# A decode layer on one core: half of the V loads move to a second DMA queue, and a selector matmul goes from the tail

## The chip, the cores and the metric

The kernel runs on one core of a Trainium2 chip. The core has a matrix engine (TensorE, PE in the profile), three engines for element-wise work (VectorE or DVE, ScalarE or ACT, GpSimd or POOL), a sync engine that here only issues transfers (SyncE, SP), and 16 DMA engines that move data between the device memory and the core's own memory. The metric is the device time of one execution in microseconds. Three runs of the kernel before gave 203.14, 202.99 and 204.5; the median is 203.14.

## The reference, cut to what matters

One token goes through one transformer layer: an attention block with a cache of 4096 positions in 32 heads, and a gated feed-forward block, each with a layer norm ahead and a residual sum behind.

```python
x = A_x                                              # [1, 1, 640]
# A: q = ln(x) @ wq -> 32 heads of 128; k_cache, v_cache: [1, 32, 4096, 128]
s = einsum("bhqd,bhkd->bhqk", q, k) * 128 ** -0.5
o = einsum("bhqk,bhkd->bhqd", softmax(s), v)
h = x + o.reshape(1, 1, 4096) @ wo                   # wo: [4096, 640]
# B: w_gate, w_up: [640, 1728], w_down: [1728, 640]
g, u = ln(h) @ w_gate, ln(h) @ w_up
out = h + (gelu(g) * u) @ w_down                     # gelu in its tanh form
```

Everything is bfloat16. The K and V caches are 32 MB each, the weights some 16 MB together, and each byte is used once.

## The kernel before, in words

**Groups and slots.** The 32 heads are taken in eight groups of four, so K of a group (K0 to K7) and V of a group (V0 to V7) are 4 MB each, laid out as 128 partitions of 32 KB. They go through three buffers of the core's memory, `slot0` to `slot2`. The list `order` (lines 170 to 173) is K0, V0, K1, then K(G+1), V(G) for G from 1 to 6, and V7; the n-th entry uses slot n % 3. `consumed[n]` is the event at which entry n has been read to its end: for K the last of four multiplies of VectorE (line 273), for V the last matmul of `pv_group` (line 310). A load of entry n waits for `consumed[n - 3]`. So V2, for example, goes into K2's slot, and K4 into V1's.

**Issue.** `issue` (line 183) writes the loads into SyncE's instruction list, in the order of `order`. Each engine works its list off in order, and a transfer that waits for a slot holds back what stands behind it in the same list. All loads of K, V and the weights are issued by SyncE, on its one DMA queue; ScalarE issues only x, at the start, on its own.

**Attention.** For each K group, `scores` makes four units of 32 positions per partition. VectorE multiplies K by q (line 273), TensorE folds the products with an identity (line 281), VectorE sums the rest (line 288), and ScalarE takes the exponentials in four parts (line 292). VectorE's list has the reduction of a unit behind the multiply of the next one. For each V group, `pv_group` multiplies the exponentials with V on TensorE (line 310), and ScalarE copies the result out (line 314). V of a group comes one K group later in the order than its own K, so TensorE takes V(G) behind the folds of K(G+1).

**Tail.** Behind V7, SyncE's list has w_o in three parts (from the arena that held w_q), then w_down's last rows, w_gate, w_up in two parts, and the rest of w_down in four. `proj_part`, the second layer norm, `glu` and the GELU follow each part. The 1728 rows of w_down make 13 and a half blocks of 128. The last half block, rows 1664 to 1727, is loaded as halves of rows on 128 partitions; the 64 GLU values that belong to it stand on partitions 0 to 63 of column 13, and a matmul with the selector `sel2` (line 451) with a multiply by `par` (line 453) spreads them into `hm2`. The last block of `down` reports one event for each of four output pieces of 160 columns (line 459), which VectorE and ScalarE copy to `out_row`.

Of the kernel before, what the change touches and what calls it, by code (L numbers as in the profile page):

```python
# [5 lines left out]
FP32 = mybir.dt.float32  # L6
BF16 = mybir.dt.bfloat16
ALU = mybir.AluOpType
ACTF = mybir.ActivationFunctionType
AX = mybir.AxisListType  # L10
# [10 lines left out]
NG = 8  # L21
NSLOT = 3
# [79 lines left out]
def bass_sequential_preLN__gqa_block_cached__glu_gated_geglu__decode_kernel(nc, A_x, A_k_cache, A_v_cache, A_wq, A_wo, B_x, B_w_gate, B_w_up, B_w_down, out):  # L102
    sb = lambda name, shape, dt: nc.alloc_sbuf_tensor(name, shape, dt)
# [10 lines left out]
    out_row = sb("out_row", [1, D], BF16)  # L114
# [5 lines left out]
    hlnT = sb("hlnT", [128, 5], BF16)  # L120
# [10 lines left out]
    e_t = sb("e_t", [128, 14], FP32)  # L131
    gu = sb("gu", [128, 14], FP32)
    hm = sb("hm", [128, 14], BF16)
    hm2 = sb("hm2", [128, 2], BF16)
    sel2 = sb("sel2", [64, 64, 2], BF16)
    par_t = sb("par_t", [128, 2, 64], BF16)
    par = sb("par", [128, 2], FP32)
    one_bf = sb("one_bf", [1, 1], BF16)
    ones_f = sb("ones_f", [128, 128], FP32)
    mean_f = sb("mean_f", [128, 128], FP32)  # L140
    ones_b = sb("ones_b", [128, 1024], BF16)
# [6 lines left out]
    ps_g, ps_u = bank[0], bank[1]  # L148
    ps_q = [bank[3], bank[7]]
    ps_a = bank[3]  # L150
    ps_d = bank[3][:, 256:416]
    ps_o = [bank[2], bank[4]]
    ps_s = bank[5]
    ps_z = bank[6]
# [5 lines left out]
    P = Prog(nc)  # L160
    V = lambda fn, *d: P.op("vector", fn, *d)
    A = lambda fn, *d: P.op("scalar", fn, *d)
    T = lambda fn, *d: P.op("tensor", fn, *d)
    GP = lambda fn, *d: P.op("gpsimd", fn, *d)
# [9 lines left out]
    pos = {t: n for n, t in enumerate(order)}  # L174
    landed, consumed = {}, {}
# [3 lines left out]
    def wo_load(name, t, lo, hi):  # L179
        d_wo[name] = P.dma("sync", wo_sb[:, t, lo:hi, :],  # L180
                           A_wo[2048 * t:2048 * t + 2048, :].rearrange("(p i) n -> p i n", i=16)[:, lo:hi, :], qd)

    def issue(upto):
        while state["next"] < min(upto, len(order)):
            n = state["next"]
            kind, g = order[n]
            src = A_k_cache if kind == "K" else A_v_cache
            src = src[0, 4 * g:4 * g + 4, :, :].rearrange("h (p r) d -> (h p) (r d)", p=32)
            dst = slots[n % NSLOT][:, 0:128 * DH]
            parts = 2 if n == len(order) - 1 else 1  # L190
            w = 128 * DH // parts
            landed[n] = [P.dma("sync", dst[:, i * w:(i + 1) * w], src[:, i * w:(i + 1) * w], consumed[n - NSLOT] if n >= NSLOT else None)
                         for i in range(parts)]
            state["next"] = n + 1

    issue(NSLOT)


# [5 lines left out]
    c_onesb = GP(lambda e: e.memset(ones_b[:, :], 1.0))  # L204
    c_idb = GP(lambda e: e.affine_select(id_b[:, :], ones_b[:, 0:128], pattern=[[1, 128]], compare_op=ALU.is_equal,
                                         fill=0.0, base=0, channel_multiplier=-1), c_onesb)
    c_idf = GP(lambda e: e.affine_select(id_f[:, :], ones_f[:, :], pattern=[[1, 128]], compare_op=ALU.is_equal,
                                         fill=0.0, base=0, channel_multiplier=-1), c_ones)
    c_sel = GP(lambda e: e.affine_select(sel[:, :, :], ones_b[0:16, :].rearrange("p (a b) -> p a b", a=8),
                                         pattern=[[-1, 8], [1, 128]], compare_op=ALU.is_equal,  # L210
                                         fill=0.0, base=0, channel_multiplier=-8), c_onesb)
    GP(lambda e: e.memset(hs[:, :, :], 0.0))
    c_hs = GP(lambda e: e.affine_select(hs_t[:, :, :], ones_f[:, 0:64].rearrange("p (a b) -> p a b", a=4),
                                        pattern=[[-32, 4], [-1, 16]], compare_op=ALU.is_equal,
                                        fill=0.0, base=0, channel_multiplier=1), c_ones)
    c_sel2 = GP(lambda e: e.affine_select(sel2[:, :, :], ones_b[0:64, 0:128].rearrange("p (a b) -> p a b", a=64),
                                          pattern=[[1, 64], [0, 2]], compare_op=ALU.is_equal,
                                          fill=0.0, base=0, channel_multiplier=-1), c_onesb)
    c_par = GP(lambda e: e.affine_select(par_t[:, :, :], ones_b[:, 0:128].rearrange("p (a b) -> p a b", a=2),
                                         pattern=[[-1, 2], [-2, 64]], compare_op=ALU.is_equal,  # L220
                                         fill=0.0, base=0, channel_multiplier=1), c_onesb)
    c_pbd = GP(lambda e: e.memset(p_bd[:, :, :, :], 0.0))
    c_rs = GP(lambda e: e.memset(RS[:, :, :], 0.0))

    c_po = [V(lambda e, b=b: e.memset(bank[b][:, :], 0.0)) for b in (2, 4)]
    c_hs = V(lambda e: e.reduce_sum(hs[:, :, 12:16], hs_t[:, :, :].rearrange("p t (g j) -> p g j t", g=4), axis=AX.X), c_hs)

    V(lambda e: e.reduce_sum(par[:, :], par_t[:, :, :], axis=AX.X), c_par)


    def x_cols(e):
# [35 lines left out]
    folds, reds, exps, pvs, evs, hds = {}, {}, {}, {}, {}, {}  # L267

    def score_mult(s):
        G, n = s // 4, pos[("K", s // 4)]  # L270
        kt = view(n)
        u = s % 4
        m = V(lambda e: e.tensor_tensor(  # L273
            out=prod[:, s % 4, :, :], in0=kt[:, 32 * u:32 * u + 32, :],
            in1=qb[:, G, :].unsqueeze(1).to_broadcast([128, 32, DH]), op=ALU.mult),
            landed[n][0], qa, qc, folds.get(s - 4))
        consumed[n] = m

        def fold(e):
            for b in range(8):  # L280
                i = e.matmul(ps_f[s % 2][:, :], id_b[:, :], prod[:, s % 4, :, 16 * b:16 * b + 16],  # L281
                             start=(b == 0), stop=(b == 7))
            return i
        folds[s] = T(fold, m, c_idb, reds.get(s - 2))
# [59 lines left out]
    def proj_part(t, lo, hi, *ws):  # L344
        def fn(e):
            for c in range(5):
                for i in range(lo, hi):
                    r = e.matmul(ps_p[:, c:c + 1], wo_sb[:, t, i, c::5], aP[:, t, i:i + 1],  # L348
                                 start=(t == 0 and c == 0 and i == 0), stop=(t == 1 and i == 15),
                                 skip_group_check=True)  # L350
            return r
        return T(fn, *ws)

    def scores(G):
        for i in range(4):
            score_mult(4 * G + i)
            if i >= 1:
                score_exp(4 * G + i - 1)
        score_exp(4 * G + 3)
        issue(pos[("K", G)] + 1 + NSLOT)  # L360

    heads = None
    for kind, G in order:
# [7 lines left out]
        if G == 4:  # L371
# [4 lines left out]
    a1 = finish_half(1)  # L376

    wo_load("0", 0, 0, 16)  # L380
    wo_load("1a", 1, 0, 12)
    wo_load("1b", 1, 12, 16)
# [4 lines left out]
    wd_sb = sl[1][:, 0:14 * D].rearrange("p (m n) -> p m n", m=14)  # L387
# [1 line left out]
    wd_v = B_w_down[0:1536, :].rearrange("(a p r) n -> p a r n", a=3, r=4)  # L389
    wd_d = wd_sb[:, 0:12, :].rearrange("p (a r) n -> p a r n", a=3)  # L390
    d_wd = [P.dma("sync", wd_sb[:, 12, :], B_w_down[1536:1664, :], free[1]),
            P.dma("sync", wd_sb[:, 13, 0:320], B_w_down[1664:1728, :].rearrange("f (s n) -> (f s) n", s=2))]
    d_wg = P.dma("sync", wg_sb, B_w_gate[:, :].rearrange("(p c) n -> p c n", c=5), free[0])
    d_wu = [P.dma("sync", wu_sb[:, 0:3, :], wu_v[:, 0:3, :]),
            P.dma("sync", wu_sb[:, 3:5, :], wu_v[:, 3:5, :])]
    d_wd += [P.dma("sync", wd_d[:, a, lo:hi, :], wd_v[:, a, lo:hi, :])
             for a, lo, hi in ((0, 0, 4), (1, 0, 4), (2, 0, 3), (2, 3, 4))]

    V(lambda e: e.memset(ps_g[64:128, 13:14], 0.0), reds[31])
    V(lambda e: e.memset(ps_u[64:128, 13:14], 0.0), reds[31])  # L400
    proj_part(0, 0, 16, a0, d_wo["0"])
    proj_part(1, 0, 12, a1, d_wo["1a"])
    pr = proj_part(1, 12, 16, d_wo["1b"])
    h = V(lambda e: e.tensor_add(hT[:, 0:5], xx[:, 0:5], ps_p[:, 0:5]), pr)  # L404
# [6 lines left out]
    def glu(ps, w, cs):  # L411
        def fn(e):
            for c in cs:
                for m in range(14):
                    ws = w[:, c, 512 * (m // 4) + m % 4:512 * (m // 4) + 512:4] if m < 12 else \
                        w[:, c, 128 * m:min(128 * m + 128, DF)]
                    i = e.matmul(ps[0:128 if m < 13 else 64, m:m + 1], ws, hlnT[:, c:c + 1],  # L417
                                 start=(c == 0 and m == 0), stop=(c == 4), skip_group_check=True)
            return i
        return fn  # L420
# [18 lines left out]
    g6 = V(lambda e: e.tensor_mul(gu[:, :], g_t[:, :], t1[:, :]), g8)  # L439
    g9 = V(lambda e: e.tensor_mul(hm[:, :], gu[:, :], ps_u[:, 0:14]), g6, up)  # L440

    def down(ms, qs=range(4)):
        def fn(e):
            for m in ms:
                for q in qs:
                    h, n = (hm[:, m:m + 1], 160 * q) if m < 13 else (hm2[:, q // 2:q // 2 + 1], 160 * (q % 2))
                    i = e.matmul(ps_d[32 * q:32 * q + 1, 0:160], h, wd_sb[:, m, n:n + 160],  # L447
                                 start=False, stop=(m == 11))
            return i
        return fn  # L450
    hp = T(lambda e: e.matmul(ps_z[:, 0:1], sel2[:, :, :].rearrange("p a b -> p (a b)"), hm[0:64, 13:14],
                              start=True, stop=True), g9, c_sel2)
    h2 = V(lambda e: e.tensor_mul(hm2[:, :], par[:, :], ps_z[:, 0:1].to_broadcast([128, 2])), hp)
    T(down([12]), d_wd[0])
    T(down(range(4)), d_wd[2])
    T(down([13]), h2, d_wd[1])
    T(down(range(4, 8)), d_wd[3])
    T(down(range(8, 11)), d_wd[4])
    dn = {q: T(down([11], [q]), d_wd[5]) for q in (0, 2, 1, 3)}
    os = [V(lambda e, q=q: e.tensor_copy(out_row[0:1, 160 * q:160 * q + 160], ps_d[32 * q:32 * q + 1, 0:160]), dn[q])  # L460
          for q in range(2)]
    os += [A(lambda e, q=q: e.copy(out_row[0:1, 160 * q:160 * q + 160], ps_d[32 * q:32 * q + 1, 0:160]), dn[q])
           for q in range(2, 4)]
    d_out = P.dma("sync", out[0, :, :], out_row[:, :], *os)
    P.op("sync", None, d_out)
# [30 lines left out]
```

## Time and profile before

| What | us |
|---|---|
| time of the profiled execution | 203.14 |
| its span, from the first to the last instruction | 201.9 |
| TensorE busy | 120.4 (60%) |
| VectorE busy | 101.2 (50%) |
| ScalarE busy | 61.1 (30%) |
| GpSimd busy | 5.0 (2%) |
| SyncE's DMA queue, share of the 16 engines' span | 97.8% |
| read from device memory | 84.23 MB, 417 GB/s over the span |

Times in the profile count from the first instruction of the span. The row named DMA gives the mean busy share of the 16 DMA engines in 40 equal slices of some 5 us, in tenths. In the timeline, the first number of a row is its start, the second its length; SPq and ACTq are the transfers that SyncE and ScalarE issue, and the length of such a row is the time that issuing took, not the transfer's. A bracket at the end tells how long the engine sat idle ahead of the row and what released it. In the chain, a DMA row's length runs from its issue to its landing. In the rows of transfers by tile, the last number is the median time from issue to landing.

### The profile page before, as it was taken

To read this page: it belongs to the slowest core of one execution; us is meant where nothing else is said; L and a number is where in the kernel's file an instruction comes from. 1 tells how busy PE (TensorE), PEld (TensorE's weight loads), DVE (VectorE), ACT (ScalarE), POOL (GpSimd) and SP (SyncE) were. 2 spreads that over 40 slices of the span, in tenths; PEclk is the share of its full clock that TensorE was granted. 3 is DMA by queue.
4 is the path that set the end of the run, shared out by engine and by line. 5 is a ranking of instruction groups with operands and counts; after the bars stand their busy time and mean duration, and the time that the engine had idled before them with its cause. 6 is when DMAs were issued, how large, how long until landed. Compare 5 with 4: busy or idle time off the path is not lost.

```text
span 201.9 us, 2505 instructions
## 1 busy us (share of the span) xinstructions
PE 120.4 (60%) x1010; PEld 58.8 (29%) x1010; DVE 101.2 (50%) x106; ACT 61.1 (30%) x273; POOL 5.0 (2%) x14
## 2 busy tenths in 40 slices
PE   0107058537937668690968197727844887467395
PEld 0103023112312233150324032312331344267383
DVE  3201088517979847924791578277708760100221
ACT  2101004620563550670156125603640363100101
POOL 7200000000000000000000000000000000000000
PEclk9999657995799996997599859988995799955555
DMA  9999999999999999999999999999999999999992
GB/s 357 414 404 467 428 415 416 422 448 458 430 415 422 415 445 448 435 424 416 422 435 441 438 435 424 416 428 441 448 419 435 399 425 437 419 408 435 412 409 113
DMA packets 4335, 84.39 MB, mean 418 GB/s; under 512 B 482, under 2 KB 868, under 8 KB 1508
## 3 DMA queue, kind: packets, MB, share of 16 engines
q1 hardware_dynamic: 4322, 84.23, 97.8%
q8 instruction: 8, 0.13, 0.3%
q14 instruction: 3, 0.02, 0.0%
q10 hardware_dynamic: 2, 0.00, 0.0%
HBM read 84.23 MB, written 0.00 MB: 417 GB/s over the span
## 4 chain that ended last, share of the span: by engine, by line
DMA 64%; PE 16%; DVE 14%; issue 3%; SPq 2%
DMA slot<-in_A_k_cache_dram 42%; DVE prod L273 12%; DMA slot<-in_B_w_down_dram 11%; DMA slot<-in_A_v_cache_dram 11%; PE bank L281 11%; PE bank L310 3%; SPq L51 2%; DVE sc L288 2%; PE bank L319 1%; PE bank L447 0%; DVE out_row L460 0%; PE bank L330 0%; DVE RT L329 0%
## 5 line engine op out<-in xcount | busy, mean ns | idle before, releaser
L281 PE MATMUL bank<-prod,id_b 128*128 128x512 bf16 x256 | 75.4, 454 | 50.8 <-DVE prod L273 50.8
L273 DVE TENSOR_TENSOR prod<-slot,qb 128x4096 bf16<-128x4096 bf16 x32 | 72.4, 2285 | 31.1 <-DMA slot<-in_A_k_cache_dram 31.1
L292 ACT ACTIVATE p_bd<-sc,zero_t 32x32 bf16<-32x32 f32 x128 | 46.4, 362 | 86.3 <-DVE sc L288 85.1
L281 PEld LDWEIGHTS bank<-prod,id_b 128*128 128x128 bf16 x256 | 26.9, 113 | 99.4 <-DVE prod L273 63.1
L288 DVE TENSOR_REDUCE sc<-bank 128x32 f32<-128x512 f32 x32 | 22.0, 688 | 21.4 <-PE bank L281 21.4
L292 ACT ACTIVATION_READ_ACCUMULATOR p_bd<-sc,zero_t 32x1 f32 x128 | 23.5, 184 | 0.0
L310 PE MATMUL bank<-slot,p_bd 128*16 128x512 bf16 x256 | 17.3, 379 | 3.1 <-ACT p_bd L292 2.5
L310 PEld LDWEIGHTS bank<-slot,p_bd 128*16 128x16 bf16 x256 | 9.4, 89 | 7.3 <-ACT p_bd L292 3.0
L319 PE MATMUL bank<-po_sb,hs 128*16 128x128 f32 x64 | 8.4, 274 | 1.1 <-ACT po_sb L314 1.1
L348 PE MATMUL bank<-aP,arena 128*128 128x1 bf16 x160 | 6.7, 178 | 3.8 <-DMA arena<-in_A_wo_dram 3.8
L417 PE MATMUL bank<-hlnT,slot 128*128 128x1 bf16 (+1 forms) x140 | 6.7, 176 | 3.2 <-DMA slot<-in_B_w_gate_dram 3.2
L259 PE MATMUL bank<-arena,xlnB 128*32 128x512 bf16 x40 | 3.9, 565 | 7.2 <-DMA arena<-in_A_wq_dram 7.2
L348 PEld LDWEIGHTS bank<-aP,arena 128*128 128x128 bf16 x160 | 6.6, 131 | 3.9 <-DMA arena<-in_A_wo_dram 2.5
L314 ACT COPY po_sb<-bank 128x512 f32<-128x512 f32 x8 | 4.7, 585 | 9.6 <-PE bank L310 9.6
L417 PEld LDWEIGHTS bank<-hlnT,slot 128*128 128x128 bf16 (+1 forms) x140 | 6.3, 118 | 4.1 <-DVE hX L407 3.3
L319 PEld LDWEIGHTS bank<-po_sb,hs 128*16 128x16 f32 x64 | 5.5, 96 | 4.5 <-issue 2.1
L244 ACT ACTIVATE ln<-ln,eps_t 128x1 f32<-128x1 f32 x2 | 0.6, 294 | 20.3 <-DVE ln L242 20.3
L263 DVE CAST qb<-bank 128x512 bf16<-128x512 f32 x1 | 0.7, 692 | 9.6 <-PE bank L259 9.6
L404 DVE TENSOR_TENSOR hT<-xx,bank 128x5 f32<-128x5 f32 x1 | 0.2, 163 | 10.2 <-PE bank L348 10.2
L233 PE MATMUL bank<-one_bf,x_row 1*128 1x1 bf16 x5 | 0.4, 177 | 6.9 <-DMA x_row<-in_A_x_dram 6.9
L259 PEld LDWEIGHTS bank<-arena,xlnB 128*32 128x32 bf16 x40 | 1.6, 136 | 9.1 <-issue 9.0
L334 DVE TENSOR_SCALAR aT<-bank,rz 16x128 bf16<-16x128 f32 x2 | 0.7, 339 | 6.0 <-PE bank L319 6.0
(65 smaller groups left out, 26.3 us busy)
## 6 DMA issues: line engine op xcount, KB each, us to landing
slot<-in_A_k_cache_dram SPq DMA_DIRECT2D x8, 4096.0 KB, 21.4
slot<-in_A_v_cache_dram SPq DMA_DIRECT2D x7, 4096.0 KB, 17.5
arena<-in_A_wq_dram SPq DMA_DIRECT2D x1, 5120.0 KB, 15.4
slot<-in_A_v_cache_dram SPq DMA_DIRECT2D x2, 2048.0 KB, 20.0
arena<-in_A_wo_dram SPq DMA_DIRECT2D x1, 2560.0 KB, 27.3
slot<-in_B_w_gate_dram SPq DMA_DIRECT2D x1, 2160.0 KB, 16.3
arena<-in_A_wo_dram SPq DMA_DIRECT2D x1, 1920.0 KB, 31.5
slot<-in_B_w_up_dram SPq DMA_DIRECT2D x1, 1296.0 KB, 18.4
```

The lines of the kernel that those rows point to most:

```text
L51: ev = self.op(eng, lambda e: e.dma_start(out, in_), *deps, dma=True)
L259: i = e.matmul(ps_q[hf][32 * j:32 * j + 32, :], xlnB[:, c, :], wq_j[:, c, j, 4 * hf:4 * hf + 4, :], start=(c == 0), stop=(c == 4))
L263: qa = V(lambda e: e.tensor_copy(qb[:, 0:4, :].rearrange("p g d -> p (g d)"), ps_q[0][:, :]), qd)
L273: m = V(lambda e: e.tensor_tensor(out=prod[:, s % 4, :, :], in0=kt[:, 32 * u:32 * u + 32, :], in1=qb[:, G, :].unsqueeze(1).to_broadcast([1 ...
L281: i = e.matmul(ps_f[s % 2][:, :], id_b[:, :], prod[:, s % 4, :, 16 * b:16 * b + 16], start=(b == 0), stop=(b == 7))
L288: reds[s] = V(lambda e: e.reduce_sum(sc[:, s % 4, :], ps_f[s % 2][:, :].rearrange("p (g d) -> p g d", d=16), axis=AX.X), folds[s], exps.ge ...
L292: x = A(lambda e, j=j: e.activation(p_bd[32 * j:32 * j + 32, G % 2, 32 * (s % 4):32 * (s % 4) + 32, j], sc[32 * j:32 * j + 32, s % 4, :], ...
L310: i = e.matmul(po[a:a + 16, :], p_bd[:, G % 2, 4 * b:4 * b + 4, :].rearrange("p g j -> p (g j)"), vt[:, 4 * b:4 * b + 4, :], start=(b < 4) ...
L314: evs[G] = A(lambda e: e.copy(po_sb[:, G % 2, :], po[:, :]), pvs[G], hds.get(G - 2))
L319: i = e.matmul(ps_a[0:16, 128 * (G // 4):128 * (G // 4) + 128], hs[:, r, 12 - 4 * g:28 - 4 * g], po_sb[:, G % 2, 128 * r:128 * r + 128], s ...
L348: r = e.matmul(ps_p[:, c:c + 1], wo_sb[:, t, i, c::5], aP[:, t, i:i + 1], start=(t == 0 and c == 0 and i == 0), stop=(t == 1 and i == 15), ...
L417: i = e.matmul(ps[0:128 if m < 13 else 64, m:m + 1], ws, hlnT[:, c:c + 1], start=(c == 0 and m == 0), stop=(c == 4), skip_group_check=True)
```

## The change

V1 to V6 are loaded through ScalarE's queue; K, V0, V7 and all weights stay on SyncE's. The load is written into ScalarE's list at the place where `issue` is called. In `scores`, that call moves from the end to a place behind the fourth multiply, ahead of the exponentials of the third and the fourth unit. The slots and what a load waits for are the same.

The last half block of w_down is loaded as the last 128 rows, 1600 to 1727, of which partitions 64 to 127 are used. `glu` writes its column 13 to these partitions, so the selector, `par`, `hm2` and their instructions are gone, two on GpSimd and one on VectorE at the start among them. Block 13 goes directly behind block 12, and the last block reports one event for all four output pieces.

```diff
@@ issue
-            landed[n] = [P.dma("sync", dst[:, i * w:(i + 1) * w], src[:, i * w:(i + 1) * w], consumed[n - NSLOT] if n >= NSLOT else None)
+            queue = "scalar" if kind == "V" and 0 < g < NG - 1 else "sync"
+            landed[n] = [P.dma(queue, dst[:, i * w:(i + 1) * w], src[:, i * w:(i + 1) * w], consumed[n - NSLOT] if n >= NSLOT else None)
@@ constants
-    c_sel2 = GP(lambda e: e.affine_select(sel2[:, :, :], ones_b[0:64, 0:128].rearrange("p (a b) -> p a b", a=64),
...
-    c_par = GP(lambda e: e.affine_select(par_t[:, :, :], ones_b[:, 0:128].rearrange("p (a b) -> p a b", a=2),
...
-    V(lambda e: e.reduce_sum(par[:, :], par_t[:, :, :], axis=AX.X), c_par)
@@ scores
             score_mult(4 * G + i)
+            if i == 3:
+                issue(pos[("K", G)] + 1 + NSLOT)
             if i >= 1:
                 score_exp(4 * G + i - 1)
         score_exp(4 * G + 3)
-        issue(pos[("K", G)] + 1 + NSLOT)
@@ tail
-            P.dma("sync", wd_sb[:, 13, 0:320], B_w_down[1664:1728, :].rearrange("f (s n) -> (f s) n", s=2))]
+            P.dma("sync", wd_sb[:, 13, :], B_w_down[1600:1728, :])]
...
-    V(lambda e: e.memset(ps_g[64:128, 13:14], 0.0), reds[31])
-    V(lambda e: e.memset(ps_u[64:128, 13:14], 0.0), reds[31])
+    V(lambda e: e.memset(ps_g[0:64, 13:14], 0.0), reds[31])
+    V(lambda e: e.memset(ps_u[0:64, 13:14], 0.0), reds[31])
...
-                    i = e.matmul(ps[0:128 if m < 13 else 64, m:m + 1], ws, hlnT[:, c:c + 1],
+                    i = e.matmul(ps[0 if m < 13 else 64:128, m:m + 1], ws, hlnT[:, c:c + 1],
...
-    hp = T(lambda e: e.matmul(ps_z[:, 0:1], sel2[:, :, :].rearrange("p a b -> p (a b)"), hm[0:64, 13:14],
-                              start=True, stop=True), g9, c_sel2)
-    h2 = V(lambda e: e.tensor_mul(hm2[:, :], par[:, :], ps_z[:, 0:1].to_broadcast([128, 2])), hp)
-    T(down([12]), d_wd[0])
-    T(down(range(4)), d_wd[2])
-    T(down([13]), h2, d_wd[1])
-    T(down(range(4, 8)), d_wd[3])
-    T(down(range(8, 11)), d_wd[4])
-    dn = {q: T(down([11], [q]), d_wd[5]) for q in (0, 2, 1, 3)}
+    T(down([12, 13], False), g9, d_wd[0], d_wd[1])
+    T(down(range(4), False), d_wd[2])
+    T(down(range(4, 8), False), d_wd[3])
+    T(down(range(8, 11), False), d_wd[4])
+    dn = T(down([11], True), d_wd[5])
```

More of the change, by code (lines that the diff above doesn't have):

```diff
@@ L133, in bass_sequential_preLN__gqa_block_cached__glu_gated_geglu__decode_kernel @@
     hm = sb("hm", [128, 14], BF16)
[L134 to L137, printed above, removed]
     one_bf = sb("one_bf", [1, 1], BF16)
@@ L215, in bass_sequential_preLN__gqa_block_cached__glu_gated_geglu__decode_kernel @@
                                         fill=0.0, base=0, channel_multiplier=1), c_ones)
-    c_sel2 = GP(lambda e: e.affine_select(sel2[:, :, :], ones_b[0:64, 0:128].rearrange("p (a b) -> p a b", a=64),
-                                          pattern=[[1, 64], [0, 2]], compare_op=ALU.is_equal,
-                                          fill=0.0, base=0, channel_multiplier=-1), c_onesb)
-    c_par = GP(lambda e: e.affine_select(par_t[:, :, :], ones_b[:, 0:128].rearrange("p (a b) -> p a b", a=2),
-                                         pattern=[[-1, 2], [-2, 64]], compare_op=ALU.is_equal,
-                                         fill=0.0, base=0, channel_multiplier=1), c_onesb)
     c_pbd = GP(lambda e: e.memset(p_bd[:, :, :, :], 0.0))
@@ L440, in bass_sequential_preLN__gqa_block_cached__glu_gated_geglu__decode_kernel, with down @@
     g9 = V(lambda e: e.tensor_mul(hm[:, :], gu[:, :], ps_u[:, 0:14]), g6, up)
-    def down(ms, qs=range(4)):
+    def down(ms, last):
         def fn(e):
             for m in ms:
[L445 to L448, printed above, removed]
-            return i
-        return fn
-    hp = T(lambda e: e.matmul(ps_z[:, 0:1], sel2[:, :, :].rearrange("p a b -> p (a b)"), hm[0:64, 13:14],
-                              start=True, stop=True), g9, c_sel2)
-    h2 = V(lambda e: e.tensor_mul(hm2[:, :], par[:, :], ps_z[:, 0:1].to_broadcast([128, 2])), hp)
-    T(down([12]), d_wd[0])
-    T(down(range(4)), d_wd[2])
-    T(down([13]), h2, d_wd[1])
-    T(down(range(4, 8)), d_wd[3])
-    T(down(range(8, 11)), d_wd[4])
-    dn = {q: T(down([11], [q]), d_wd[5]) for q in (0, 2, 1, 3)}
-    os = [V(lambda e, q=q: e.tensor_copy(out_row[0:1, 160 * q:160 * q + 160], ps_d[32 * q:32 * q + 1, 0:160]), dn[q])
+                k = slice(0 if m < 13 else 64, 128)
+                for q in range(4):
+                    i = e.matmul(ps_d[32 * q:32 * q + 1, 0:160], hm[k, m:m + 1], wd_sb[k, m, 160 * q:160 * q + 160],
+                                 start=False, stop=(last and m == ms[-1]))
+            return i
+        return fn
+    T(down([12, 13], False), g9, d_wd[0], d_wd[1])
[3 more added lines that the diff above has]
+    dn = T(down([11], True), d_wd[5])
+    os = [V(lambda e, q=q: e.tensor_copy(out_row[0:1, 160 * q:160 * q + 160], ps_d[32 * q:32 * q + 1, 0:160]), dn)
           for q in range(2)]
-    os += [A(lambda e, q=q: e.copy(out_row[0:1, 160 * q:160 * q + 160], ps_d[32 * q:32 * q + 1, 0:160]), dn[q])
+    os += [A(lambda e, q=q: e.copy(out_row[0:1, 160 * q:160 * q + 160], ps_d[32 * q:32 * q + 1, 0:160]), dn)
            for q in range(2, 4)]
```

## The prediction

> **What bounds the kernel now.** I read the page's DMA rows first, then the chain that ended last, then the SyncE rows of the timeline. The page:
>
> ```profile
> span 201.9 us, 2505 instructions
> ...
> DMA  9999999999999999999999999999999999999992
> ...
> q1 hardware_dynamic: 4322, 84.23, 97.8%
> ...
> q10 hardware_dynamic: 2, 0.00, 0.0%
> ```
>
> One queue (q1, SyncE's) keeps the 16 DMA engines busy from the first slice to the last but one; ScalarE's queue (q10) carries two packets. No compute engine exceeds 60%. So the kernel ends when its last byte lands, and a change can cost time in three ways only: more bytes, a pause in the stream, or a longer tail behind the last byte. The chain in order of time gives the pace:
>
> ```profile
> 1.65 42.91 DMA slot<-in_A_k_cache_dram
> ...
> 73.81 19.85 DMA slot<-in_A_k_cache_dram
> ...
> 111.10 21.41 DMA slot<-in_A_k_cache_dram
> ...
> 149.22 22.22 DMA slot<-in_A_v_cache_dram
> ...
> 176.80 22.42 DMA slot<-in_B_w_down_dram
> ```
>
> K of group 1 lands at 44.56 (1.65 + 42.91), K of 4 at 93.66, K of 6 at 132.51. Four 4 MB loads lie between the last two (V3, K5, V4, K6), so one takes 38.85 / 4 = 9.71 us; five lie between 44.56 and 93.66 (K2, V1, K3, V2, K4), 9.82 each. Transfers run one behind another without a pause, although SyncE issues each only when a slot comes free:
>
> ```profile
> 43.22 0.33 SPq L51 DMA_DIRECT2D slot<-in_A_v_cache_dram  x1
> 56.43 0.33 SPq L51 DMA_DIRECT2D slot<-in_A_k_cache_dram  x1
> 69.12 0.33 SPq L51 DMA_DIRECT2D slot<-in_A_v_cache_dram  x1
> 73.81 0.33 SPq L51 DMA_DIRECT2D slot<-in_A_k_cache_dram  x1
> ```
>
> ```profile
> 74.25 4.49 DVE L273 TENSOR_TENSOR prod<-slot,qb 128x4096 bf16<-128x4096 bf16 x2 [2.47 <-DMA slot<-in_A_k_cache_dram]
> ```
>
> The first four rows are the issues of V1, K3, V2 and K4; the fifth, VectorE's, is the start on K3 when it lands, at 74.25. V2's issue at 69.12 comes 5.1 us before the stream would run dry at 74.25: that is the cover which the change has to keep. Three more prices follow. K3 is read to its end at 85.82, the issue of V3, 11.6 after it landed (K4 likewise: 93.66 to 105.38, 11.7). V1's slot comes free 73.81 - 69.12 = 4.7 after K2's. And K2, which found VectorE busy with K1, was done 69.12 - 56.43 = 12.7 after it.
>
> **The change, part by part.** *V1 to V6 on ScalarE's queue.* Nothing is added to the bytes here; what changes is the order. In before, V1 is served behind K2, because both are in one queue. After, V1 is issued by ScalarE behind V0's eviction, 43.22 + 0.58, before K1 lands, so K2 and V1 are due at the same moment on two queues. How do the engines serve two queues? The one pair in this trace is x on q10 beside w_q on q1:
>
> ```profile
> 1.29 0.50 ACTq L51 DMA_DIRECT2D x_row<-in_A_x_dram  x1
> ```
>
> ```profile
> L233 PE MATMUL bank<-one_bf,x_row 1*128 1x1 bf16 x5 | 0.4, 177 | 6.9 <-DMA x_row<-in_A_x_dram 6.9
> ...
> arena<-in_A_wq_dram SPq DMA_DIRECT2D x1, 5120.0 KB, 15.4
> ```
>
> x is issued at 1.29, behind w_q (issued at 0.00), and is used at 6.93, while w_q lands at 15.4: the second queue is let in within a transfer of the first. The trace's packet records are finer still: x's data packet runs at 5.00, its 4-byte completion packet at 6.57, and between them fits one w_q packet of 1.51 us. That is taking turns, packet by packet. A V load has as many packets per engine as a K load, of equal size, so I take half of the rate for each.
>
> The Trainium skill bears on both sides of this. "DMA: Bandwidth & Descriptors", section "Queues, rings and completion order", says that an engine goes round its queues in turn and leaves one only after a whole packet, typically 9 to 17 descriptors. If a K load's share of one engine were one such packet, K2 would still land before V1, and the sum below would be +0.2 us. The row of x, let in long before w_q's end, speaks for the fine grain. The same page's section "Issuing engines are not separate DMA queues" says that all queues interleave on the same engines and that a second issuer saves only issue time; by that nothing is gained here, and the loss that I find is not foreseen.
>
> Now the walk. From 44.56, K2 and V1 share two loads' time, 19.4 us. K2 lands at 44.56 + 19.4 = 64.0 if its last packet comes last, at 62.8 if one packet (9.71 / 8 = 1.2) earlier; before, one load behind K1, it was near 54.5. VectorE has been done with K1 since about 59, so it waits. K3, issued at 56.4 on SyncE's queue, follows as the third load and lands at 74.2, as before: the stream is full until there. K2 is read to its end 11.7 after landing, at 74.5 to 75.7, and only then is V2 issued. K4 needs V1's slot, 4.7 later still. So at 74.2 **both queues are empty** and all three slots hold data being read: the 5.1 us of cover become a shortfall of 0.3 to 1.5 us, plus the restart.
>
> The restart r, from issue to the moment from which the load counts at full rate, was hidden and is now in the open. Below: the output's store, 1.2 KB on an idle queue, issued in 0.31 and then awaited by SyncE for 0.8: 1.1 us. Above: w_q, issued at 0.00, landed at 15.4, of which 5.12 MB at the pace above take 12.1: 3.3 us, program start included. V2 is neither; it is a load as large as w_q, in a program already running. I take 2.2. Pause: 75.1 + 2.2 - 74.2 = **3.1 us**, between 74.5 + 1.1 - 74.2 = 1.4 and 75.7 + 3.3 - 74.2 = 4.8.
>
> Does it come again? V2 runs alone from 77.3, K4 (issued at 79.8) joins 4.7 later, so the queues are now out of step: V2 is done at 92.0, K4 at 101.4, V3 at 111.4, and K5 then has 4.7 left, to 116.1. K4 is read out at 113.1; V4 is in flow at 115.3. The cover is 0.8 us, or -0.3 with the long restart. The same step falls again between K7 and V6, near 154. I take 0 for both and leave 0 to 0.6 for the range.
>
> A pause also lets the DMA engine that lags catch up: the five loads up to 93.66 took 49.10 against 5 x 9.71 = 48.55. That is worth 0 to -0.55; I take -0.2.
>
> *ScalarE's six issues.* 0.33 us each as on SyncE, 0.50 as x took: 2 to 3 us in six places. ScalarE waits there for the fourth multiply of a K group, with the exponentials of the third and fourth unit behind it. Those need a reduction that VectorE runs after that same multiply, so the wait costs nothing; an exponential is used only one group later. 0.
>
> *w_down's tail.* The second load grows from 80 to 160 KB: 0.08 MB at 418 GB/s, +0.2 us on the stream. The selector matmul and `hm2` (two steps of 0.18 and 0.16 us) leave a stretch in which PE is waiting for w_down anyway, from 197.24 to the last landings near 199.6: 0. Still 56 matmuls. The last four report one event in place of four; in before the copies started at 200.01 and 200.04 while PE was done at 199.98, so 0 to +0.1, taken at 0.1. The GpSimd and VectorE work taken from the start (0.70, 0.29 and 0.29 us, over by 5.5) ends before x arrives at 6.93: 0.
>
> Sum: 3.1 - 0.2 + 0.2 + 0.1 = **+3.2 us**. The profiled execution took 203.14 for a span of 201.9, and is itself the median of the three runs. Forecast: 203.1 + 3.2 = 206.3.
>
> **Rivals.**
> 1. *K keeps its place* (ends on the other side: not slower). If SyncE's queue gets more than its half, K2 lands earlier. There is no pause if K2 is read out r before 74.2: it must land by 74.2 - 11.7 - 1.1 = 61.4 with the short restart, by 59.2 with the long one. K2's 9.71 us in 16.8 or 14.6 us: a share of 58% to 66%. From there on the price is 0.2 + 0.1: 203.4. For it: a 5.1 us cover to spare. Against it: x's turn-taking.
> 2. *The pause recurs.* K5 and K7 have 0.8 us of cover or less. If a read-out takes 12.7 in place of 11.7 (as back to back), or the restart is the long one, each costs 0.3 to 1.5, on a first pause of 3 to 4.8: +5 to +6, 208 to 209.
> 3. *Two queues fill gaps.* q1 is busy 97.8%; the missing 2.2% are 4.4 us, of which the last slice (at 113 GB/s, some 3.5 us) is the tail that no queue fills. At most 1 us is left: 202.1 with no pause at all. More than 1% faster would need bytes to move faster than 9.71 us a load, for which nothing in the trace speaks.
>
> **How the numbers follow.** One pause as walked: 0.74. Rival 1: 0.11. Rival 2: 0.11. Rival 3, and anything that makes it faster: 0.04. A change of 1%, 2 us, is about what a measurement of this kernel can tell from none (its own runs spread from 202.99 to 204.5). One pause at its low end (1.4 to 1.8) lies within 1%; that is 0.11 of its 0.74. So faster 0.03, same 0.23, slower 0.74. The range runs from rival 1's 203.4 to the top of rival 2, 209.0.
>
> **What would show it.** In the changed profile: V1 and K2 land within 1.5 us of each other near 63 to 64; VectorE waits some 4 us for K2 where it had K2 at hand before; one slice of the DMA row near 74 to 78 falls well below 9, and the GB/s with it; V2's issue on ScalarE's queue at about 75; from there all lags by some 3 us, to the end; the last landing to the end takes no more than 0.2 longer than now. I am wrong if K2 lands by 61 (rival 1), if the DMA row dips at three places (rival 2), or if 4 MB take other than 9.7 us where both queues run.

## The result, and the profile after

The changed kernel takes 209.28 us (median of 6 runs, 208.87 to 211.11) against 203.14 us before: 6.1 us more, a ratio of 1.0303 with a 95% interval of 1.0255 to 1.0351. The forecast was 206.3 with a range of 203.3 to 209.0: the direction was right, the size half of what came, and the time lies just above the range. Medians here are over all runs of a kernel, while ratios leave out runs that lie more than 1.5% above the kernel's fastest, so the two can differ, by up to 0.9%.

The page of the changed kernel, the rows that were read first of before:

```profile
span 208.1 us, 2498 instructions
...
DMA  9999999999999789999999999999979999999992
GB/s 355 394 455 403 447 447 416 409 476 422 405 453 447 321 302 413 460 430 409 447 453 384 384 414 441 441 416 441 428 280 403 409 409 430 426 413 432 409 410 101
...
q1 hardware_dynamic: 3458, 59.15, 66.7%
q10 hardware_dynamic: 866, 25.17, 29.0%
```

A slice is 5.2 us. The stream dips at three places: slices 14 and 15 (321 and 302 GB/s), 22 and 23 (384 each), and 30 (280), which is 68 to 78, 109 to 120 and 151 to 156 us. Before had nothing of the kind. The two queues together are busy 95.7%, where q1 alone had been 97.8%.

The chain that ended last, in order of time, its DMA rows:

```profile
36.90 24.71 DMA slot<-in_A_k_cache_dram
...
77.86 23.29 DMA slot<-in_A_k_cache_dram
...
118.58 23.99 DMA slot<-in_A_k_cache_dram
...
159.35 17.83 DMA slot<-in_A_v_cache_dram
...
181.81 23.63 DMA slot<-in_B_w_down_dram
```

K2 lands at 36.90 + 24.71 = 61.6, 7 us later than before. The last half of V7 lands at 177.18 in place of 171.44, 5.7 us late, and the last but one part of w_down at 205.44 in place of 199.22, 6.2 us late. So 5.7 us are lost before the weights of the tail, and the tail itself adds some 0.5.

Where the 5.7 us went is read from three stretches. The columns that matter are the last two, the busy share of the DMA engines and GB/s. The changed kernel:

```profile
62.00:82.00 20.00, 15.27 (x88) 6.56 (x88) 17.28 (x12) 8.26 (x39) 0.00 (x0) 0.87 0.90 371
104.00:122.00 18.00, 15.29 (x89) 6.54 (x88) 14.83 (x13) 7.99 (x38) 0.00 (x0) 0.89 0.99 411
146.00:164.00 18.00, 14.88 (x86) 6.26 (x84) 15.12 (x11) 8.79 (x41) 0.00 (x0) 0.92 0.89 368
```

The kernel before, in the same stretches:

```profile
62.00:82.00 20.00, 14.97 (x86) 6.29 (x84) 14.77 (x11) 8.29 (x39) 0.00 (x0) 0.91 1.02 435
104.00:122.00 18.00, 11.64 (x69) 4.86 (x67) 10.33 (x10) 6.35 (x30) 0.00 (x0) 0.81 0.99 425
146.00:164.00 18.00, 10.78 (x67) 4.85 (x67) 11.25 (x8) 5.93 (x28) 0.00 (x0) 0.81 1.00 427
```

At some 430 GB/s the bytes missing in each stretch are worth 20 x (435 - 371) / 430 = 3.0 us, 18 x 14 / 430 = 0.6 us and 18 x 59 / 430 = 2.5 us: 6.1 us together, good to a few tenths, against the 5.7 us of the chain. The trace also keeps start, length and size of every packet that a DMA engine moved, and these packet records give the sum in another way: between 5 and 170 us the 16 engines are without a data packet for 4.1 us in the mean (0.04 us in the kernel before), and the packets with which V2, V4 and V6 restart the stream are longer, by some 2.0 us in sum for each engine. The first pause has the size forecast (2.9); the other two had been put at nothing.

The pauses hang on V2, V4 and V6, each issued when a K group has been read to its end. ScalarE's issues, and VectorE's start on K2:

```profile
73.17 0.33 ACTq L51 DMA_DIRECT2D slot<-in_A_v_cache_dram  x1
112.87 0.33 ACTq L51 DMA_DIRECT2D slot<-in_A_v_cache_dram  x1
154.30 0.34 ACTq L51 DMA_DIRECT2D slot<-in_A_v_cache_dram  x1
```

```profile
61.64 4.49 DVE L262 TENSOR_TENSOR prod<-slot,qb 128x4096 bf16<-128x4096 bf16 x2 [2.84 <-DMA slot<-in_A_k_cache_dram]
```

By the trace's landing records, the load ahead of each (K3, K5, K7) lands at 74.08, 115.71 and 156.01. So V2, V4 and V6 are issued 0.9, 2.8 and 1.7 us before the stream's last landing, where before V2 led by 5.1 and V4 and V6 by 7.7 and 7.8.

### The profile page after: what moved, and what is told of

Its sections match the earlier page's. It is cut to its first block, busy times and chain, and to the rows that moved or that the text cites. A ratio compares the mean times of both kernels' runs of the same rounds, so it can differ in the third digit from the quotient of the medians.

```text
span 208.1 us, 2498 instructions
## 1 busy us (share of the span) xinstructions
PE 116.9 (56%) x1009; PEld 56.2 (27%) x1009; DVE 100.3 (48%) x104; ACT 61.1 (29%) x273; POOL 4.1 (2%) x12
## 4 chain that ended last, share of the span: by engine, by line
DMA 66%; PE 14%; DVE 14%; issue 2%; SPq 2%
DMA slot<-in_A_k_cache_dram 46%; DVE prod L262 12%; DMA slot<-in_B_w_down_dram 11%; PE bank L270 10%; DMA slot<-in_A_v_cache_dram 9%; PE bank L299 3%; DVE sc L277 2%; SPq L51 2%; PE bank L308 1%; PE bank L436 0%; DVE out_row L445 0%; PE bank L319 0%; DVE RT L318 0%
## 5 line engine op out<-in xcount | busy, mean ns | idle before, releaser
L270 PE MATMUL bank<-prod,id_b 128*128 128x512 bf16 x256 | 69.9, 426 | 54.4 <-DVE prod L262 54.4
L270 PEld LDWEIGHTS bank<-prod,id_b 128*128 128x128 bf16 x256 | 25.2, 107 | 99.4 <-DVE prod L262 68.0
L299 PE MATMUL bank<-slot,p_bd 128*16 128x512 bf16 x256 | 18.1, 406 | 8.6 <-DMA slot<-in_A_v_cache_dram 6.1
L299 PEld LDWEIGHTS bank<-slot,p_bd 128*16 128x16 bf16 x256 | 8.3, 93 | 15.3 <-DMA slot<-in_A_v_cache_dram 7.3
```

The lines of the kernel that those rows point to most:

```text
L299: i = e.matmul(po[a:a + 16, :], p_bd[:, G % 2, 4 * b:4 * b + 4, :].rearrange("p g j -> p (g j)"), vt[:, 4 * b:4 * b + 4, :], start=(b < 4) ...
```

## The experiments

Theory: K is served beside V and lands late, is read out late, and the slot that the next V load needs comes free when the stream is dry or nearly so. Rivals: a price for each load on the second queue, a share of the tail, or ScalarE held up. L numbers in the rows of each experiment are those of its own source.

### The two parts by themselves

The queue move alone: before, with

```diff
+            queue = "scalar" if kind == "V" and 0 < g < NG - 1 else "sync"
-            landed[n] = [P.dma("sync", ...
+            landed[n] = [P.dma(queue, ...
```

and the earlier place of `issue` in `scores`.

> The queue move alone: V1 to V6 through ScalarE's queue and the earlier place of issue, with the old tail of w_down. Theory (pauses of the stream: K2 lands late beside V1, so V2 is issued after the stream ran dry, and the same at K5/V4 and K7/V6): nearly all of the loss is here, +5.5 to +6.0 us on 203.14, so about 208.9, with three dips of the DMA row near 74, 114 and 154 us. Rival (the tail holds a part of the loss that the pauses do not explain): +3 to +5 us, 206 to 208.

210.12 us, ratio 1.0331 (1.0263 to 1.04), with the pauses at the same three places:

```profile
DMA  9999999999999789999999799999989999999992
```

The tail alone: the changed kernel with `queue = "sync"`.

> The changed kernel with all loads on SyncE's queue, so only the new tail of w_down is left. Theory: 0.2 us for 80 KB more and up to 0.1 us for the single event of the last block: 203.3 to 203.5, no dip of the DMA row. Rival (the tail holds a part of the loss): 204 to 206.

203.58 us, ratio 1.0028 (0.9994 to 1.0061). The whole loss is the queue's; the tail costs 0.3 us by the medians, as its bytes would, and the interval does not tell that from nothing. The profiled run of the second kernel (205.27) was one of four in twelve that took over 205, and it has a small dip, 366 GB/s in the slice from 71 to 76 us, where none was expected; the last experiment returns to it.

### Which load meets which

```diff
-            queue = "scalar" if kind == "V" and 0 < g < NG - 1 else "sync"
+            queue = "scalar" if kind == "V" and g == 1 else "sync"
```

> Only V1 on ScalarE's queue, V2 to V6 back on SyncE's; new tail. Theory (one collision, K2 with V1): K2 lands at about 61.6 in place of 54.5, V2 is issued at about 73, one pause of 2.6 us as in the changed kernel up to K5, none after it: 203.1 + 2.6 + 0.3 = 206.0. Rival (each load on the second queue has a price of its own, a sixth of 5.8 us): 203.1 + 1.0 + 0.3 = 204.4.

206.47 us (205.07 to 206.88), ratio 1.0118 (1.0079 to 1.0156). The profiled run, the shortest of the nine, has one dip:

```profile
DMA  9999999999999979999999999999999999999992
```

One load in six on the second queue brings half of the loss. With `1 < g < NG - 1` in place of `g == 1`:

> V2 to V6 on ScalarE's queue, V1 on SyncE's; new tail. Theory (the loss hangs on which load meets which, not on the number of loads on the second queue): K2 lands near 54.5 as before, V2 is issued near 69 while K3 is still in transfer, no pause near 74; later K loads are late beside V loads, with at most small pauses near 114 and 154: 203.5 to 206. Rival (a price for each load on the second queue, five sixths of 5.8 us): 208.2.

205.28 us (203.42 to 208.64), ratio 1.0043 (0.9999 to 1.0086). Five loads in six cost less than the one, and the profiled run, 203.61 us, has no dip behind its start; V2, V4 and V6 are issued 8.0, 7.7 and 6.3 us before K3, K5 and K7 land:

```profile
DMA  8999999999999999999999999999999999999992
```

A price for each load is ruled out. The wide spread may mean that the collisions behind K4 and K6 are near an edge in this kernel, but none of its long runs was profiled, so this is not shown.

### When K is read to its end

The four multiplies of a K group first, the reductions behind them; the multiplies, folds and reductions themselves are unchanged.

```diff
 def scores(G):
-        for i in range(4):
-            score_mult(4 * G + i)
...
+        ms = [score_mult(4 * G + i) for i in range(4)]
+        issue(pos[("K", G)] + 1 + NSLOT)
+        for i in range(4):
+            if i >= 2:
+                score_exp(4 * G + i - 2)
+            score_fold(4 * G + i, ms[i])
+        score_exp(4 * G + 2)
+        score_exp(4 * G + 3)
```

> The changed kernel with VectorE's four multiplies of a K group back to back, the reductions behind them: K is read to its end some 9.2 us after landing in place of 11.7, so its slot is free 2.5 us earlier. Theory (pauses come from a slot that comes free after the stream ran dry): all or most of each pause of 1.5 to 2.6 us goes, 203.5 to 205. Rival (the second queue costs by itself, or ScalarE is held up): unchanged, 209.3.

204.35 us (203.19 to 206.69), ratio 1.0027 (0.9994 to 1.006). Four fifths of the loss are gone by the medians, nine tenths by the ratios, with all six V loads still on the second queue. In the same three stretches of the profiled run (205.28), the second and third pause are gone (425 and 422 GB/s), and of the first one 20 x (435 - 409) / 430 = 1.2 us are left:

```profile
62.00:82.00 20.00, 16.18 (x88) 7.01 (x88) 17.49 (x11) 7.15 (x33) 0.00 (x0) 0.80 0.97 409
```

The same edit in the kernel before is the control.

> The four multiplies first, in the kernel before: the control to the same edit in the changed kernel. Theory: the stream is full already, so nothing is gained or lost, 203.0 to 203.3. Rival (the order of VectorE's work has a value of its own): 1 us or more either way.

203.26 us (203.0 to 203.42, ten runs), ratio 0.9997 (0.9984 to 1.001).

The opposite edit holds K longer: in groups 2, 4 and 6 the last multiply is done twice.

```diff
+        if u == 3 and G in (2, 4, 6):
+            m = V(lambda e: e.tensor_tensor(
+                out=prod[:, s % 4, :, :], in0=kt[:, 32 * u:32 * u + 32, :],
+                in1=qb[:, G, :].unsqueeze(1).to_broadcast([128, 32, DH]), op=ALU.mult), m)
         consumed[n] = m
```

> The changed kernel with K of groups 2, 4 and 6 read 2.28 us longer: the last multiply of the group is done twice with the same values, and the slot is free after the second. Theory: the three pauses each grow by about 2.3 us, 209.3 + 6.9 = 216.2. Rival (pauses are not set by when K is read to its end; VectorE is idle for half of the span): 209.3 to 210.

215.72 us (212.45 to 217.55), ratio 1.0523 (1.0431 to 1.0615). That is 6.4 us more than the changed kernel by the medians and 4.5 by the ratios; 6.9 were expected. In the profiled run, the longest of the four, the DMA row dips in three places, to two, four and four tenths where the changed kernel has seven, nine and seven:

```profile
DMA  9899899999999289999994799999948999999992
```

In the kernel before, the same three extra multiplies:

> The same longer reading of K2, K4 and K6 in the kernel before. Theory: there each V load is issued 5 to 8 us before the stream would run dry, so 2.3 us are covered: 203.1 to 203.4. Rival (any delay of VectorE reaches the end): 205 to 210.

204.92 us (204.15 to 204.99), ratio 1.0067 (1.0044 to 1.009), so 1.4 to 1.7 us. That is a miss, on a stretch that was thought to be covered by 5.1 us. V2 is issued at 70.16 here, 1.0 us later than before and 3.9 us ahead of K3's landing, and yet the stream thins out:

```profile
72.00:76.00 4.00, 2.79 (x41) 1.91 (x40) 2.57 (x2) 2.65 (x12) 0.00 (x0) 1.00 0.99 360
```

Before had 463 GB/s in these 4 us. V4 and V6 are issued 3.2 and 3.6 us later than before, but still 5.3 and 5.4 us ahead of the landings of K5 and K7, and their stretches stay at 427 and 420 GB/s. Side by side, one profiled run each, kernels in which K3 lands at 74.0 to 74.3:

| Kernel | V2 issued, us | GB/s, 72 to 76 us |
|---|---|---|
| multiplies first for K1 and K2 (the last experiment) | 67.03 | 459 |
| multiplies first, before | 67.14 | 492 |
| before | 69.12 | 463 |
| tail alone | 70.12 | 328 |
| K held, before | 70.16 | 360 |
| multiplies first, after | 71.01 | 369 |
| V1 alone | 72.24 | 270 |
| after | 73.17 | 164 |
| queue move alone | 73.29 | 139 |

So short a stretch scatters, and can lie above the 432 GB/s of a full stream, but the step is plain: with a lead of 5 us or more over K3's landing the stream stays full, with 4 us it thins, and with 1 us it stops. So before's own cover was not 5.1 us; it was about 1 or less.

### How two queues share an engine

K2 to K7 in four DMAs of 8 KB for each partition, all awaited before the first multiply; V with its 32 KB packets.

```diff
-            parts = 2 if n == len(order) - 1 else 1
+            parts = 2 if n == len(order) - 1 else 4 if kind == "K" and g >= 2 else 1
...
-            landed[n][0], qa, qc, folds.get(s - 4))
+            *landed[n], qa, qc, folds.get(s - 4))
```

> The changed kernel with K2 to K7 loaded in four DMAs of 8 KB for each partition, all awaited before the first multiply; V keeps its 32 KB packets. Theory (an engine takes turns packet by packet): beside a V load K gets 8 of 40 KB, a fifth of the rate, so K2 lands near 63.5 to 64 in place of 61.6, the K loads behind it are late too, and the pauses grow: 212 to 216. Rival (turns by bytes or by time): K keeps its half, 209 to 210.

221.42 us (221.16 to 221.76), ratio 1.0896 (1.0862 to 1.0929): the theory's direction, and more than its size. K2's last quarter lands at 64.7, V1 at 61.6; by the packet records, in stretches of 2 us between 48 and 60 us q1 moves 70 to 107 GB/s and q10 295 to 475, about one to four. The size follows from the issues: V2, V4 and V6 are issued 1.9, 2.0 and 1.7 us after K3, K5 and K7 land, where the changed kernel issues them 0.9, 2.8 and 1.7 us before. That is 11 us later in sum, and the 8 KB packets add some 1.5 us (worked out below); 12.1 us more than in the changed kernel were measured. VectorE's wait for K2 grows from 2.84 us to:

```profile
64.84 2.29 DVE L262 TENSOR_TENSOR prod<-slot,qb 128x4096 bf16<-128x4096 bf16 x1 [6.86 <-DMA slot<-in_A_k_cache_dram]
```

The converse, with `kind == "V" and g >= 1`:

> The converse: V1 to V6 in four DMAs of 8 KB for each partition, K with 32 KB packets. Theory: K gets four fifths of the rate beside a V load, K2 lands near 56, V2 is issued near 70 and the pauses near 114 and 154 us go: 203.5 to 205.5, with both queues as busy as in the changed kernel. Rival (turns by bytes or by time): 209 to 210.

205.17 us (204.58 to 205.8), ratio 1.0096 (1.0063 to 1.013). From 48 to 54 us q1 moves 295 to 426 GB/s and q10 74 to 102, about four to one. K2 lands at 56.7, and no pause is left; the two queues carry the same bytes as in the changed kernel:

```profile
DMA  9999999999999999989998999999989999999992
...
q10 hardware_dynamic: 3458, 25.17, 29.7%
```

The third experiment of this kind puts the parts that keep the stream full together: the old tail, multiplies first, V1 to V6 on ScalarE's queue in 8 KB packets.

> The kernel before with V1 to V6 on ScalarE's queue in 8 KB packets, and VectorE's four multiplies of a group first; old tail of w_down. Theory: with every slot free some 3 us ahead of need, the second queue costs and brings nothing: 203.0 to 203.5. Rival (a second queue has a small price of its own beside the pauses): 204 to 205.5.

204.53 us (204.45 to 204.7), ratio 1.0066 (1.0044 to 1.0088), so 1.5 us above before: the theory's range is missed, and the time lies in the rival's. There is no pause in this run either:

```profile
DMA  9999999998999999989998998999989999999992
```

The eights of the last two DMA rows are not idle time: by the packet records the engines are without a data packet for 0.1 us in the mean between 5 and 170 us, in either run. The 8 KB packets can account for the 1.5 us: the records give 0.312 us for one, where a quarter of a 32 KB packet (1.213 us) is 0.303; 3072 of them on 16 engines make 192 x 0.009 = 1.7 us. This is an estimate, since no run has such packets on one queue. That the second queue has no price of its own, to a few tenths, is seen with 32 KB packets in the shortest runs: four of the ten runs of the changed kernel with the multiplies first took 203.19 to 203.50, and three of the ten with V2 to V6 on the second queue 203.42 to 203.61, where the tail alone has a median of 203.58.

### Before's own edge

Before ran at 203.0 to 203.4 in most runs, and at 203.7 to 205.8 in the others: in 10 of the 28 runs beside the first four experiments, 6 of 20 beside the four with the reading of K, 1 of 9 beside the three with 8 KB packets, and 1 of the 16 beside this one. If V2's issue sits at an edge, two groups of the better order should be enough to end that: the multiplies first for K1 and K2 alone.

```diff
 def scores(G):
+        if G not in (1, 2):
...                                      # the order of before
+            return
         ms = [score_mult(4 * G + i) for i in range(4)]
```

> The kernel before with the four multiplies first for K1 and K2 alone, so that V2 alone is issued some 2 us earlier. Some runs of the kernel before take 204 to 206 in place of 203.1. Theory (V2's issue at 69 to 70 us is at the edge of what keeps the stream full, and a slower clock in K1 pushes it over): all runs lie within 203.0 to 203.5, as with the edit in all groups. Rival (those runs come from something else, and the edit in the other groups removed it): a third of the runs still at 204 to 206.

203.18 us, eleven runs, all from 202.97 to 203.51; before beside it, 203.13 with runs up to 205.31; ratio 1.0002 (0.9993 to 1.0011). V2 is issued at 67.03 and the stretch is full:

```profile
72.00:76.00 4.00, 1.99 (x35) 1.21 (x26) 1.77 (x2) 2.92 (x13) 0.00 (x0) 1.00 1.07 459
```

The median is that of before, so nothing here is faster than before by its median. No run is long, but with only one long run in 16 of before beside it, this experiment alone could hardly tell. Together with the control above, in which all groups have the multiplies first, it is none of 21 runs against 7 of 36 of before beside them. That is unlikely to be chance, but that the earlier V2 is the cause is not shown. What makes V2 late in a single run is open too, since no long run of before itself was profiled. The one long run of its order that was, the tail alone, speaks against a slower clock in K1: there VectorE starts on K2 at 58.45, ahead of the 59.01 of before, and falls behind only in K2, whose third multiply starts at 65.02 (before: 64.01); the granted TensorE clock from 62 to 68 us is 0.81, in before 1.00.

## Why the prediction was right and wrong, point by point

- **The bound, and the mechanism: right.** The kernel lives on an unbroken stream. V1 beside K2 makes K2 land late, so V2's slot comes free too late. Reading K out earlier takes most of the loss away, reading it out later adds loss, and giving K four fifths of the bytes removes the pauses. K2 landed at 61.6 where 62.8 to 64.0 was walked: V1 joins some 3 us after its issue, so K2 had a start alone.
- **The first pause: right in size, by luck.** 2.9 us forecast with what the lagging engine gives back, 3.0 measured from the bytes. But with K2 early, V2 was issued at 73.17 and not at 75.1, and by the prediction's own sum the pause would then have been 73.17 + 2.2 - 74.08 = 1.3 us. The early issue and the lead that was taken too short (next point) made up for each other.
- **"Does it come again?": the step that failed.** The walk found K5 and K7 nearly where they came (K5 at 116.1, measured 115.7), and V4 in flow at 115.3, so a cover of 0.8 us; "I take 0 for both and leave 0 to 0.6 for the range". The pauses measured 0.6 and 2.5 us by the bytes. Two terms of the comparison were wrong. It set the moment at which a load counts at full rate against the *landing* of the load ahead. But the 16 engines end a load at different times, and earlier: by the packet records K5's last packets end from 113.5 to 115.4, and K7's from 153.1 to 155.7. And a load needs a lead of 4 to 5 us over that landing before nothing is lost, as the table of issue times shows; the walk used 2.2. With a need of 3.7 us, a value fitted to the sum, the three leads of 0.9, 2.8 and 1.7 give pauses of 2.8, 0.9 and 2.0, in sum 5.7. K in 8 KB packets, to which it was not fitted, agrees: issues 1.9, 2.0 and 1.7 us after the landings give 16.7 us of pauses, and 203.0 + 0.3 + 1.5 + 16.7 = 221.5 us, measured 221.42. It is not a sharp limit: for the lead of 3.9 us in the kernel before with K held it gives no loss, and 1.4 to 1.7 us were lost.
- **"The 5.1 us of cover": wrong for the same reason.** It was mostly not cover. Holding K 2.3 us longer in the kernel before, which moved V2's issue by only 1.0 us, cost 1.4 to 1.7 us.
- **Rival 2** (the pause recurs, 208 to 209) is what happened, with 0.11 of the chance; the time came out just above its range. Its two places, K5 and K7, were named. Of its two conditions the longer read-out did not come (K4 landed at 101.15 and V4 was issued at 112.87, 11.7 us later); the longer restart did.
- **Rival 1** is refuted by the three dips, rival 3 by the time. K2's landing alone would not have settled it: 61.6 is only 0.2 us behind the 61.4 up to which rival 1 saw no pause with the short restart, and 3.0 us were lost. Its condition was then made by an edit, V in 8 KB packets: with four fifths of the bytes for K there are no pauses.
- **ScalarE's six issues: right, nothing on the path.** They take 0.33 to 0.36 us, and in the runs in which the stream stays full no price of theirs is seen.
- **w_down's tail: right,** 0.3 us alone by the medians, not clear of noise.
- **"4 MB take 9.7 us where both queues run": right.** The packets keep their 1.213 us while the two queues alternate.

On the Trainium skill, "DMA: Bandwidth & Descriptors", section "Queues, rings and completion order": turns by packet are what the two experiments with 8 KB packets show, with one byte in five for the queue with the small packets. But in these runs a turn is one row of a partition, 8 or 32 KB, not a group of 9 to 17 descriptors. Section "Issuing engines are not separate DMA queues" is borne out in that nothing was gained, but moving loads between issuers was not neutral: it changed who lands first, and cost 6.1 us.

## What to carry to other kernels

Where one queue feeds a pipeline through a few slots, its order is part of the design: a second queue lets a transfer that is needed later take turns with the one that is needed next, packet by packet, and then every slot comes free late. Judge the cover of a stream by the lead of an issue over the time the engines run dry, not over the landing; here a lead of 4 us was already too little for 4 MB loads in 32 KB packets. When a walk leaves less cover than the restart that it has just priced, forecast the pause, not its absence.

## What was not expected of the hardware

- A load that joins busy engines waits: V1, issued at 43.28, has its first packet at 46.72 by the records, and x, in the kernel before, issued at 1.29, at 5.00: 3.4 and 3.7 us. On idle engines V2's first packet came 1.0 us after its issue (73.17 to 74.15) and took 1.7 to 2.1 us in place of 1.21.
- The landing is queued too. K1's last packet ends at 44.16 and it lands at 44.61. K2's, beside V1, ends at 59.93 and it lands at 61.61: 1.7 us in place of 0.5. The records show why: each engine ends a load with a packet of 4 bytes, and K2's last of these runs at 61.13, behind one packet of V1 (1.2 us), as x's did behind one of w_q; K1's ran at 44.16, at once.
- With a change of a few us in VectorE's order, which left the median as it was, none of 21 runs took over 203.6, where 7 of 36 of before took 203.7 to 205.3. The cause is open.
